# A bank for each transpose: q and k of the early chunks write to PSUM banks of their own

## The chip, the cores and the metric

The kernel runs on one core of a Trainium2 chip. The core has five engines with a queue of instructions each: TensorE (PE: matmuls and transposes, with its weight loads shown as PEld), VectorE (DVE), ScalarE (ACT), GpSimd (POOL) and SyncE (SP, which here only issues DMAs). Engines tell each other through semaphores. The metric is the device time of one execution in microseconds (us); less is better. PSUM, where TensorE writes, has eight banks in this kernel's book-keeping: five that the plan hands out one by one (bank 0 to bank 4), two for scores (the tile `sc`) and one for the state (the tile `st`).

## The reference

A gated linear attention feeds a two-layer block with a squared ReLU. Inputs are q, k, v and alpha of shape 4 x 8 x 768 x 48 (batch, heads, sequence, head dimension) and two weights, 384 x 2048 and 2048 x 384.

```python
for t in range(S):
    state = alpha[:, :, t, :, None] * state + np.einsum('bhd,bhe->bhde', k[:, :, t], v[:, :, t])
    y[:, :, t] = np.einsum('bhd,bhde->bhe', q[:, :, t], state)
x = y.transpose(0, 2, 1, 3).reshape(B * S, H * D)
h = x @ w_in
return (np.maximum(h, 0.0) ** 2) @ w_out
```

## The kernel before

**Tiles.** The 3072 tokens are cut into 24 chunks of 128 tokens, six to a batch element. The state is carried from one chunk to the next; within a chunk the recurrence is done with matmuls: cumulative sums of log alpha (`p0`), their exponentials `A` and `Ainv`, the products qA = q * A and kI = k * Ainv (L522, L528, L727), their transposes (`p1q` and `p1k`; in a double chunk `p1`), scores q k (`p2`) with a mask (`sm`), the state's update (`ps`, then `stm` and the copy `sb`), and the output (`p3a` from the old state, `p3b` from the scores), which is copied as `xn`, transposed once more (`p4`), and copied into `xT_big` as the input of the block. The block takes tokens in groups: the first of four chunks, two of one, then nine of two. `moe1` is x @ w_in with the ReLU on ACT (L915) and the square on DVE (L923); `moe2` is the product with w_out.

**Double chunks.** The first four chunks are done as two double chunks (`add_super`, L661): 256 tokens, in two halves of four heads each (v = 0 and 1). Each half has its own `p0`, products, transposes and copies. Chunks 4 to 23 are done one by one (`add_chunk`, L454). Chunks 4 and 5 (s below EARLY = 6) copy q and k out of PSUM with two instructions, either on ACT or on DVE; chunks 6 to 9 with one on DVE; from chunk 10 on the transposes are made by DMAs and take no PSUM.

**What sets the order.** Every step is an `Op` with an engine, a duration, the steps it depends on and a priority. `Plan.run` places them one at a time at the earliest time that its own durations give, and the instructions are then issued in the order of the planned starts. On the chip each engine goes through its queue in that order. An op may take a bank (`takes`) from a list of `Slots`; the bank comes free when the op in `gives` is done. The bank lists are `GLA_BANKS` (banks 0 and 1, for single chunks), `SUP_BANKS` (banks 0 to 3, for double chunks) and the last three for the block. Where the plan leaves TensorE idle before the first `moe2`, matmuls on a tile of zeros (`idle_mm`, tile `warm`) are put in.

**Around the change.** The four transposes of q and the four of k of one half (or of one chunk) each write 128 x 512 bf16 values, one kilobyte a partition, which is half of a bank; both go into one tile `pT` of 128 x 1024, a whole bank. q's are issued first, then k's. The copies (`cast`, L418, on ACT L420 and on DVE L422) bring each part to the tile `qkT`. The bank is given back by the copy of k. The semaphores are placed by the language's layer under the kernel: as built, the transposes of k wait for the copy of q where that copy was issued first, and the copy of q waits for the transposes of k where those were issued first.

Of the kernel before, what the change touches and what calls it, by code (L numbers as in the profile page):

```python
# [9 lines left out]
BF16 = mybir.dt.bfloat16  # L10
# [49 lines left out]
def after(op, x=0.0):  # L60
    return (op, x)
# [109 lines left out]
def kernel(  # L171
# [13 lines left out]
    P = 128  # L185
    DP = 64
    NP = H // 2
# [32 lines left out]
    HF = P // 2  # L220
# [46 lines left out]
    ident_bf = consts.tile([P, P], BF16)  # L267
# [6 lines left out]
    def pin(ins):  # L274
        tc.keep_in_program_order(ins)
# [4 lines left out]
    def tr(*a):  # L280
        pin(nc.tensor.transpose(*a))  # L281

    plan = Plan()
# [4 lines left out]
    GLA_BANKS = sl_bank[0:2]  # L288
    SUP_BANKS = sl_bank[0:4]
# [3 lines left out]
    def psum(op, shape, dt):  # L293
        i = op.slot.bank
        return banks[i].tile(shape, dt, name=f"bank{i}")
# [6 lines left out]
    def add(eng, dur, emit, *deps, **kw):  # L302
        return plan.add(Op(eng, dur, emit, deps, **kw))
# [69 lines left out]
    EARLY = 2 * 3  # L373
# [44 lines left out]
    def cast(op, out_t, in_t):  # L418
        if op.eng == "ACT":
            pin(nc.scalar.copy(out_t, in_t))  # L420
        elif op.eng == "DVE":
            pin(nc.vector.tensor_copy(out_t, in_t))  # L422
        else:
            pin(nc.gpsimd.tensor_copy(out_t, in_t))
# [29 lines left out]
    def add_chunk(s):  # L454
        d = C[s]
        b, c = divmod(s, NCH)
        i = s % NBUF
        L, qA, kI, ae = L_s[:, i], qA_s[:, i], kI_s[:, i], ae_s[:, i].rearrange("p j n -> p n j")
        was = C[s - NBUF]
        old = was["end"] if s < 2 * NS + NBUF else None  # L460
        g = dict(prio=-10.0 + s * 0.01)
# [68 lines left out]
        mk = d["use_kt"] = add("DVE", 0.47, e_kI, ai, d["ld_kt"], *([old] if old else [was["cps"][1], was.get("ps")]), **g)  # L530
# [4 lines left out]
                tr(d["pT"][:, p, :], qA[:, 2 * p:2 * p + 2, :], ident_bf)  # L535

        def e_p1k():
            for p in range(NP):
                tr(d["pT"][:, NP + p, :], kI[:, 2 * p:2 * p + 2, :], ident_bf)
        def e_turn():  # L540
            d["qkT"] = work.tile([P, 2 * NP, P], BF16, name="qkT")
            pin(nc.sync.dma_start_transpose(out=d["qkT"], in_=qk_s[:, i].rearrange("p x h d -> p (x h d)")))
        if s < XFROM:
            p1q = plan.add(Op("PE", 0.22, e_p1q, [mq], takes=GLA_BANKS, **g))
            p1k = plan.add(Op("PE", 0.22, e_p1k, [mk, after(p1q)], lat=0.15, **g))

        def e_cp(lo, hi):
            if lo == 0:
                d["qkT"] = work.tile([P, 2 * NP, P], BF16, name="qkT")
            cast(cpk if lo else cp, d["qkT"][:, lo:hi, :], d["pT"][:, lo:hi, :])  # L550
        if s < EARLY:
            cp = add({"ACT": 0.49, "DVE": 0.34}, 0, lambda: e_cp(0, NP), p1q, **g)
            cpk = add({"DVE": 0.34, "ACT": 0.49}, 0, lambda: e_cp(NP, 2 * NP), p1k, after(cp, -9.0), **g)
        elif s < XFROM:
            cp = cpk = add("DVE", 0.61, lambda: e_cp(0, 2 * NP), p1k, was["py_op"], **g)
        else:
            cp = cpk = add("XB", 0.0, e_turn, mq, mk, was["py_op"], lat=2.8)
            cp.turn = 1.2
        if s < XFROM:
            p1q.gives = cpk  # L560

        d.update(cps=[cp, cpk], mk=mk, vb_op=vb, ae1=ae1, kI=kI, ae=ae)
        if s < PAIRS:
# [97 lines left out]
    def add_super(u):  # L661

        d = SUP[u]
        i = 2 * u % NBUF
        pair = (C[2 * u], C[2 * u + 1])
        L, qA, kI, ae = L_s[:, i:i + 2], qA_s[:, i:i + 2], kI_s[:, i:i + 2], ae_s[:, i:i + 2].rearrange("p b j n -> p b n j")
        old = [C[2 * u - NBUF + ab].get("end") for ab in range(2)] if u >= 2 else []
        g = dict(prio=-10.0 + u * 0.02)
        any_ = (0, 1)
        sets = "p h s d -> p s h d"  # L670
        NH = NP // 2
# [54 lines left out]
        def e_mul(op, out, src, f):  # L726
            pin((nc.gpsimd if op.eng == "POOL" else nc.vector).tensor_mul(out, src, f))  # L727
        mq = [add("DVE", 0.47, lambda v=v: e_mul(mq[v], qA[:, :, hsl[v], 0:D], d["qt"][:, hsl[v]].rearrange(sets), d["A"][v]),
                  a_[v], d[f"ld_qt{v}"], *old, **g) for v in any_]
        mk = [add(KI_ON[u][v], 0, lambda v=v: e_mul(mk[v], kI[:, :, hsl[v], 0:D], d["kt"][:, hsl[v]].rearrange(sets), d["Ai"][v]),  # L730
                  ai[v], d[f"ld_kt{v}"], *old, **g) for v in any_]
        d["use_qt"], d["use_kt"] = mq[1], mk[1]

        d["pT"], d["qk"] = [None, None], [None, None]

        def e_p1(v, w, src):
            if w == 0:
                d["pT"][v] = psum(p1[v], [P, 2, NH, 2, 2, HF], BF16)
            for t in any_:
                for n in range(NH):  # L740
                    p = NH * v + n
                    tr(d["pT"][v][:, w, n, :, t, :], src[:, t, 2 * p:2 * p + 2, :], ident_bf)

        def e_cp(v, w):
            if w == 0:
                d["qk"][v] = work.tile([P, 2, NH, 2, 2, HF], BF16, name="qkT")
            cast((cpq, cp)[w][v], d["qk"][v][:, w], d["pT"][v][:, w])
        p1, cp, cpq = [None, None], [None, None], [None, None]
        for v in any_:
            p1[v] = plan.add(Op("PE", 0.225, lambda v=v: e_p1(v, 0, qA), [mq[v]], takes=SUP_BANKS, lat=0.15, **g))  # L750
            p1k = plan.add(Op("PE", 0.225, lambda v=v: e_p1(v, 1, kI), [mk[v], after(p1[v])], lat=0.15, **g))
            cpq[v] = add({"ACT": 0.49, "DVE": 0.34}, 0, lambda v=v: e_cp(v, 0), p1[v], **g)
            cp[v] = add({"DVE": 0.34, "ACT": 0.49}, 0, lambda v=v: e_cp(v, 1), p1k, cpq[v], **g)
            p1[v].gives = cp[v]
        cq = cp[1]

        def qT(p):
# [66 lines left out]
        for ab in any_:  # L824
            s = 2 * u + ab
# [40 lines left out]
            if s:  # L866
                p3a = c["p3a"] = plan.add(Op("PE", 0.2, e_p3a, [cq, before], takes=SUP_BANKS, **g))
            p3b = c["p3b"] = plan.add(Op("PE", 0.5, e_p3b, [*sm, *vb, after(p3a)], takes=None if s else SUP_BANKS,
                                         lat=0.15, **g))
# [140 lines left out]
    for x in DMA_ORDER + [s for s in range(2 * NS, NT) if s not in DMA_ORDER]:  # L1010
        if x in ("i", "o"):
            load_w(x)
        elif isinstance(x, str):
            for nm in x[1:].split():
                add_load2(int(x[0]), nm)
            if len(SUP[int(x[0])]) == 2 * len(srcs) - 1:
                add_super(int(x[0]))
        else:
            for nm, _ in srcs:
                add_load(x, nm)  # L1020
            add_chunk(x)
# [47 lines left out]
    for op in plan.order:  # L1069
        if op.eng == "PE":  # L1070
# [3 lines left out]
            if pe_end is not None and DUMMY:  # L1074
                cold = pe_end < COLD
                n = max(0, int((op.start - pe_end - (0.05 if cold else 0.2)) / (0.22 if cold else 0.11)))
# [32 lines left out]
```

## Time and profile before

| | |
|---|---|
| time, median of 3 runs | 178.14 us (178.06 to 179.42) |
| time of the profiled execution | 178.12 us |
| its span | 176.3 us |
| TensorE busy | 169.5 us, 96% of the span, 1854 matmuls |
| VectorE, ScalarE, GpSimd busy | 126.3, 123.1 and 53.4 us |
| granted TensorE clock | 0.999 |
| transposes of q and k on TensorE (L281) | 80, 219 ns each from start to result |
| copies of q or k, 128x512 | 10 on DVE, 422 ns each; 2 on ACT, 586 ns each |

The profile is one execution, read by the hardware profiler. Times of rows are counted from the start of the span. A row of the timeline has the start, the time from the first start to the last end of a run of equal instructions, the engine, the line, what is written and read, the number of instructions, and in brackets how long the engine was idle before and what ended that. A row of the waits has who waited, for whom, the total in us, how often, and the longest. The time of an execution is some 1.8 us more than its span.

### The profile page before, as it was taken

The page shows a single profiled execution, that of the slowest core. Times are in us where ns is not written, and L with a number is a line of the kernel's source. Part 1 is how long each engine was busy: PE and PEld are TensorE (multiplying, and loading weights), DVE is VectorE, ACT ScalarE, POOL GpSimd, SP SyncE. Part 2 cuts the span into 40 slices and gives each one's busy share as a digit, 9 for nine tenths or more (in the row PEclk, how much of TensorE's full clock was granted, in tenths as well). Part 3 has the DMA queues.
Part 4 walks back from the last instruction along what each step waited for, and adds up shares of the span by engine and source line. Part 5 has one row for each costly group of instructions (what it writes and reads, how often), then busy time and mean ns, then how long its engine had stood idle before and what let it go on. Part 6 is the DMA issues. An engine that isn't in the chain of part 4 may idle for free.

```text
span 176.3 us, 4803 instructions
## 1 busy us (share of the span) xinstructions
PE 169.5 (96%) x1854; PEld 125.0 (71%) x1854; DVE 126.3 (72%) x259; ACT 123.1 (70%) x266; POOL 53.4 (30%) x97
## 2 busy tenths in 40 slices
PE   7779999999999999999999999999999999999993
PEld 2457794566897788866786786785878866867863
DVE  6678889957799798869699777789486741820600
ACT  4569779446898679983899499695797833743821
POOL 6120779911121101032332213303328278200000
PEclk9999999999999999999999999999999999999999
DMA  5999999899989989999999996998989899822012
GB/s 132 274 283 301 382 387 369 175 224 204 223 176 179 212 163 179 179 179 214 199 168 214 178 199 135 142 226 152 192 157 196 215 199 325 306 45 93 0 45 89
DMA packets 117206, 34.86 MB, mean 198 GB/s; under 512 B 111952, under 2 KB 114640, under 8 KB 117184
## 3 DMA queue, kind: packets, MB, share of 16 engines
q1 hardware_dynamic: 115200, 31.21, 84.1%
q0 software_dynamic: 1984, 3.36, 6.2%
q8 instruction: 14, 0.23, 0.6%
q14 instruction: 8, 0.07, 0.1%
HBM read 25.17 MB, written 4.72 MB: 170 GB/s over the span
## 4 chain that ended last, share of the span: by engine, by line
PE 85%; DVE 6%; ACT 6%; issue 2%; DVEq 0%; ACTq 0%
PE bank L278 77%; PE bank L281 4%; PE sc L278 3%; PE st L278 2%; ACT r L915 2%; DVE sm L597 1%; DVE gT L923 1%; DVE qk_s L727 1%; ACT xn L420 1%; DVE qk_s L528 1%; ACT A L711 1%; DVE qkT L422 1%; ACT sb L847 1%; ACT Af L494 0%; ACT Ainv L711 0%
## 5 line engine op out<-in xcount | busy, mean ns | idle before, releaser
L278 PE MATMUL bank<-xT_big,w_in_b 128*128 128x256 bf16 (+2 forms) x606 | 72.2, 267 | 0.0
L278 PE MATMUL bank<-w_out_b,gT 128*128 128x384 bf16 (+2 forms) x400 | 68.8, 319 | 0.0
L915 ACT ACTIVATE r<-bank 128x512 bf16<-128x512 f32 (+1 forms) x97 | 56.5, 603 | 10.9 <-PE bank L278 8.6
L923 DVE TENSOR_TENSOR gT<-r 128x512 bf16<-128x512 bf16 (+1 forms) x97 | 47.2, 520 | 18.4 <-ACT r L915 17.9
L278 PEld LDWEIGHTS <-w_in_b 128*128 128x128 bf16 x606 | 53.3, 98 | 9.8
L278 PEld LDWEIGHTS <-gT 128*128 128x128 bf16 x400 | 37.4, 98 | 20.1
L470 POOL CAST vb<-vt 128x384 bf16<-128x384 f32 x20 | 10.6, 528 | 45.6 <-DMA vt<-in_v_dram 20.1
L991 ACT COPY held<-bank 128x384 f32<-128x384 f32 x21 | 10.1, 481 | 18.6 <-PE bank L278 17.3
L511 POOL DMA_DIRECT2D ae_s<-Af x24 | 12.1, 509 | 36.2 <-ACT Af L494 36.1
L597 DVE TENSOR_TENSOR sm<-sc,utri_b 128x512 bf16<-128x512 f32 x24 | 15.4, 683 | 2.8 <-PE sc L278 2.7
L525 DVE TENSOR_TENSOR qk_s<-qt,Af 128x384 bf16<-128x384 f32 x12 | 10.3, 856 | 6.4 <-ACT Af L494 6.3
L420 ACT CAST xn<-bank 128x384 bf16<-128x384 f32 x24 | 11.2, 484 | 4.7 <-PE bank L278 4.6
L278 PEld LDWEIGHTS <-qkT 64*128 64x128 bf16 (+2 forms) x304 | 10.6, 97 | 4.3 <-issue 1.9
L528 DVE TENSOR_TENSOR qk_s<-kt,Ainv 128x384 bf16<-128x384 f32 x20 | 11.7, 585 | 0.8 <-ACT Ainv L498 0.5
L465 ACT ACTIVATE L_s<-at 128x384 bf16<-128x384 f32 x20 | 10.7, 534 | 0.9 <-DMA at<-in_alpha_dram 0.9
L494 ACT ACTIVATE Af<-bank 128x384 f32<-128x384 f32 x12 | 10.6, 883 | 1.0 <-PE bank L278 0.5
L498 ACT ACTIVATE Ainv<-bank 128x384 bf16<-128x384 f32 x20 | 10.4, 519 | 0.0
L631 DVE TENSOR_TENSOR st<-st,ae_s 128x384 f32<-128x384 f32 x16 | 8.9, 558 | 1.9 <-ACT xn L420 1.1
L597 DVE TENSOR_TENSOR sm<-bank,utri_b 128x512 bf16<-128x512 f32 x16 | 10.2, 679 | 0.0
L281 PE MATMUL bank<-ident_bf,qk_s 128*128 128x128 bf16 x80 | 7.4, 219 | 2.5 <-DVE qkT L422 0.9
L422 DVE COPY qkT<-bank 128x512 bf16<-128x512 bf16 (+1 forms) x14 | 6.8, 497 | 4.2 <-PE bank L281 4.0
L636 ACT CAST sb<-st 128x384 bf16<-128x384 f32 x16 | 7.9, 497 | 2.5 <-DVE st L631 2.5
(74 smaller groups left out, 165.7 us busy)
## 6 DMA issues: line engine op xcount, KB each, us to landing
at<-in_alpha_dram SPq DMA_DIRECT2D x24, 192.0 KB, 3.9
qt<-in_q_dram SPq DMA_DIRECT2D x24, 192.0 KB, 3.8
kt<-in_k_dram SPq DMA_DIRECT2D x24, 192.0 KB, 3.9
vt<-in_v_dram SPq DMA_DIRECT2D x20, 192.0 KB, 3.8
wo<-in_moe_w_out_dram SPq DMA_DIRECT2D x4, 768.0 KB, 6.5
out_dram<-held POOLq DMA_DIRECT2D x13, 192.0 KB, 4.5
wi<-in_moe_w_in_dram SPq DMA_DIRECT2D x4, 384.0 KB, 6.5
wi<-in_moe_w_in_dram SPq DMA_DIRECT2D x2, 768.0 KB, 8.5
```

Source lines behind the costliest of these rows:

```text
L278: pin(nc.tensor.matmul(*a, **kw))
L281: pin(nc.tensor.transpose(*a))
L420: pin(nc.scalar.copy(out_t, in_t))
L465: pin(nc.scalar.activation(L[:, :, 0:D], d["at"], AF.Ln))
L470: pin(nc.gpsimd.tensor_copy(d["vb"], d["vt"]))
L494: pin(nc.scalar.activation(d["A"], split(d["pm"][:, 0:HD], s), AF.Exp))
L498: pin(nc.scalar.activation(d["Ai"], d["pm"][:, 0:HD].rearrange("p (h d) -> p h d", h=H), AF.Exp, scale=-1.0))
L511: pin(nc.gpsimd.dma_start(out=ae_s[HF * j:HF * j + D, i, j], in_=d["Af"][P - 1:P, j]))
L528: pin(nc.vector.tensor_mul(kI[:, :, 0:D], d["kt"], d["Ai"]))
L597: pin(nc.vector.tensor_mul(d["sm"][:, hh], d["sc"][hh], utri_b.to_broadcast([P, NP, P])))
L915: pin(nc.scalar.activation(box["r"][:, 0:w], box["ph"][:, 0:w], AF.Relu))
L923: pin(nc.vector.tensor_mul(gT[g][:, f0:f0 + per, lo * P:lo * P + n], r, r))
```

## The change

Transposes of q and transposes of k now take a bank each, in both double chunks and in chunks 4 and 5, and each bank is given back by its own copy. Chunks 6 to 9 keep one bank with one copy. The work, the engines' tiles and the number of matmuls are the same; the plan is run anew with the new banks.

```diff
@@ add_chunk: chunks 4 and 5 (s < EARLY)
         def e_p1k():
+            d["pTk"] = psum(p1k, [P, NP, P], BF16) if s < EARLY else d["pT"][:, NP:]
             for p in range(NP):
-                tr(d["pT"][:, NP + p, :], kI[:, 2 * p:2 * p + 2, :], ident_bf)
+                tr(d["pTk"][:, p, :], kI[:, 2 * p:2 * p + 2, :], ident_bf)
...
-            p1k = plan.add(Op("PE", 0.22, e_p1k, [mk, after(p1q)], lat=0.15, **g))
+            p1k = plan.add(Op("PE", 0.22, e_p1k, [mk, after(p1q)], takes=GLA_BANKS if s < EARLY else None, lat=0.15, **g))
...
-            cast(cpk if lo else cp, d["qkT"][:, lo:hi, :], d["pT"][:, lo:hi, :])
+            cast(cpk if lo else cp, d["qkT"][:, lo:hi, :], d["pTk"] if lo and s < EARLY else d["pT"][:, lo:hi, :])
...
         if s < XFROM:
-            p1q.gives = cpk
+            if s < EARLY:
+                p1q.gives, p1k.gives = cp, cpk
+            else:
+                p1q.gives = cpk
@@ add_super: the double chunks
-        d["pT"], d["qk"] = [None, None], [None, None]
+        d["pT"], d["qk"] = {}, [None, None]
 
         def e_p1(v, w, src):
-            if w == 0:
-                d["pT"][v] = psum(p1[v], [P, 2, NH, 2, 2, HF], BF16)
+            d["pT"][v, w] = psum((p1, p1k)[w][v], [P, NH, 2, 2, HF], BF16)
...
-                    tr(d["pT"][v][:, w, n, :, t, :], src[:, t, 2 * p:2 * p + 2, :], ident_bf)
+                    tr(d["pT"][v, w][:, n, :, t, :], src[:, t, 2 * p:2 * p + 2, :], ident_bf)
...
-            cast((cpq, cp)[w][v], d["qk"][v][:, w], d["pT"][v][:, w])
+            cast((cpq, cp)[w][v], d["qk"][v][:, w], d["pT"][v, w])
...
-            p1k = plan.add(Op("PE", 0.225, lambda v=v: e_p1(v, 1, kI), [mk[v], after(p1[v])], lat=0.15, **g))
+            p1k[v] = plan.add(Op("PE", 0.225, lambda v=v: e_p1(v, 1, kI), [mk[v], after(p1[v])], takes=SUP_BANKS, lat=0.15, **g))
...
-            p1[v].gives = cp[v]
+            p1[v].gives, p1k[v].gives = cpq[v], cp[v]
```

As built, TensorE's queue has the same instructions. Up to the output of the double chunks their order is the same. In chunk 5 the transposes of `xn` of chunk 4 come behind one quarter of `moe2` instead of ahead of it, a few matmuls of `moe1` move past transposes and outputs of chunks 5 and 6, and one copy of `xT_big` (chunk 4) goes to DVE instead of ACT. From about chunk 8 on all five queues have the order of before, with banks 0 and 1 exchanged. No DMA changes its place.

More of the change, by code (lines that the diff above doesn't have):

```diff
@@ L746, in e_cp @@
                 d["qk"][v] = work.tile([P, 2, NH, 2, 2, HF], BF16, name="qkT")
-            cast((cpq, cp)[w][v], d["qk"][v][:, w], d["pT"][v][:, w])
-        p1, cp, cpq = [None, None], [None, None], [None, None]
+            cast((cpq, cp)[w][v], d["qk"][v][:, w], d["pT"][v, w])
+        p1, p1k, cp, cpq = [None, None], [None, None], [None, None], [None, None]
         for v in any_:
             p1[v] = plan.add(Op("PE", 0.225, lambda v=v: e_p1(v, 0, qA), [mq[v]], takes=SUP_BANKS, lat=0.15, **g))
-            p1k = plan.add(Op("PE", 0.225, lambda v=v: e_p1(v, 1, kI), [mk[v], after(p1[v])], lat=0.15, **g))
+            p1k[v] = plan.add(Op("PE", 0.225, lambda v=v: e_p1(v, 1, kI), [mk[v], after(p1[v])], takes=SUP_BANKS, lat=0.15, **g))
             cpq[v] = add({"ACT": 0.49, "DVE": 0.34}, 0, lambda v=v: e_cp(v, 0), p1[v], **g)
-            cp[v] = add({"DVE": 0.34, "ACT": 0.49}, 0, lambda v=v: e_cp(v, 1), p1k, cpq[v], **g)
-            p1[v].gives = cp[v]
+            cp[v] = add({"DVE": 0.34, "ACT": 0.49}, 0, lambda v=v: e_cp(v, 1), p1k[v], cpq[v], **g)
+            p1[v].gives, p1k[v].gives = cpq[v], cp[v]
         cq = cp[1]
```

## The prediction, on record before the run

> **What bounds the kernel now.** I read the engines' shares first, then the waits of the first 22 us, then the timeline around each transpose of q and k. The page, shares by engine and the chain that ended last:
>
> ```profile
> PE 169.5 (96%) x1854; PEld 125.0 (71%) x1854; DVE 126.3 (72%) x259; ACT 123.1 (70%) x266; POOL 53.4 (30%) x97
> ...
> PE 85%; DVE 6%; ACT 6%; issue 2%; DVEq 0%; ACTq 0%
> ```
>
> TensorE is the bound. By stretches it is busy 7.51 of the first 10 us, 8.86 of the next 10, and from 20 to 170 us between 9.83 and 10 of every 10. So a microsecond saved ahead of 20 us moves the end only if TensorE reaches its dense part earlier; behind it, only true gaps of TensorE count. The waits, 0 to 22 us, name what the change touches:
>
> ```profile
> PE bank L281 <- DVE qkT L422: 0.9, 2, 0.5
> ...
> PE bank L281 <- ACT qkT L420: 0.7, 1, 0.7
> ```
>
> L281 are transposes, L422 and L420 the copies out of PSUM: three times in the double chunks the transposes of k stand behind the copy of q, 1.6 us in all. The timeline shows each, and what comes behind:
>
> ```profile
> 6.60 0.42 DVE L422 COPY qkT<-bank 128x512 bf16<-128x512 bf16 x1
> ...
> 7.07 0.38 PE L281 MATMUL bank<-ident_bf,qk_s 128*128 128x128 bf16 x4 [0.52 <-DVE qkT L422]
> ...
> 9.63 0.56 DVE L727 TENSOR_TENSOR qk_s<-kt,Ainv 128x384 bf16<-128x384 f32 x1
> ...
> 10.09 0.59 ACT L420 COPY qkT<-bank 128x512 bf16<-128x512 bf16 x1 [0.98 <-PE bank L281]
> ...
> 10.73 0.38 PE L281 MATMUL bank<-ident_bf,qk_s 128*128 128x128 bf16 x4 [0.67 <-ACT qkT L420]
> ...
> 17.05 0.38 PE L281 MATMUL bank<-ident_bf,qk_s 128*128 128x128 bf16 x4 [0.34 <-DVE qkT L422]
> ...
> 17.65 0.51 POOL L424 CAST vb<-vt 128x384 bf16<-128x384 f32 x1 [4.53 <-DMA vt<-in_v_dram]
> ...
> 18.35 0.51 PE L278 MATMUL st<-vb,qk_s 64*128 64x96 bf16 x8
> ```
>
> The reader is to see two kinds of edges: those between engines, which the change removes, and two that a DMA sets. The product kI of the second half starts at 9.63, and its load of k, issued at 4.66, took 4.9 us: it landed at 9.56. The load of v of the second double chunk, issued at 10.73, took 6.9 us; GpSimd had waited 4.53 us for it. In chunk 5 (timeline, 36 to 62 us) no transpose waits, but the copies do, and then TensorE:
>
> ```profile
> 44.13 0.75 DVE L422 COPY qkT<-bank 128x512 bf16<-128x512 bf16 x2 [0.91 <-PE bank L281]
> ...
> 45.00 0.10 PEld L278 LDWEIGHTS <-utri_b 128*128 128x128 bf16 x1 [0.48 <-PE bank L278]
> 45.03 0.32 PE L278 MATMUL bank<-L_s,utri_b 128*128 128x384 bf16 x1
> ```
>
> The row names TensorE's own matmul as releaser, which was long done. The bank that this p0 of chunk 6 takes is the one that the two copies empty at 44.88, so I take the copies.
>
> **The change part by part.**
>
> *First double chunk, first half.* kI is ready at 6.50 (row 5.95, 0.55), so the transposes of k start at some 6.60 instead of 7.07. Of these 0.47 us at most 0.07 outlive the load of k that lands at 9.56 and starts the second half's kI at 9.63. Worth nothing.
>
> *Second half.* kI ends at 10.19; k's transposes start at 10.26 instead of 10.73, their results are there at 10.65. The copy of k then waits for DVE, whose mask of 0.68 from 10.10 ends at 10.78: 10.78 instead of 11.22, **0.44 us** ahead. All that follows to 16.11 (state, sb, exponentials, products) hangs on this copy by the chain, and its loads land at 12.9 to 15.2, ahead of it.
>
> *Second double chunk.* In its second half the copy of q no longer stands ahead of k's transposes: kI ends at 16.66, TensorE is through with its matmuls at about the same time, so 16.75 instead of 17.05, **0.3 us** more. A wait is added: the transposes of xn of chunk 1 take the bank of the first half's q, whose copy ends at 16.19, against 16.04 before; behind them stand six moe1 matmuls of 0.055 us each and k's transposes. Its cost lies between 0 and 0.2 and is in the 16.75. So the scores come some 0.7 us earlier, and then v is missing: its cast ends at 17.65 + 0.51 = 18.16 whatever the transposes do. The state's matmuls start 0.05 behind such an end (sb ends at 20.17, its reader starts at 20.22), at 18.21 instead of 18.35. From 18.35 to 20.22 TensorE's queue is back to back (state, output, moe1, then the matmuls on zeros, which stay), so **0.14 us** is what TensorE takes along into its dense part; about 0.6 us turn into waiting for v.
>
> *Chunk 4.* Its eight transposes run back to back (38.55, 0.61) and TensorE has work ahead of the scores. Its k now takes the bank of its p0, last read at 37.89 (37.72 + 0.17). Nothing.
>
> *Chunk 5.* q's transposes start at 43.49, eight take 0.44 between starts; those of q alone give their last result at 43.49 + 3 x 0.055 + 0.219 = 43.88. The copy of q starts there + 0.03 = 43.91 instead of 44.13, both copies end 0.75 later at 44.66. Meanwhile TensorE does k, a quarter of moe2 (0.65, as from 42.84 to 43.49) and the moved transposes of xn: free at 44.75. p0 of chunk 6 follows the copies by 0.15 as before, at 44.81 instead of 45.03: **0.22 us**. Two waits are added. k's transposes wait for ACT's copy of xn (43.03 + 0.48 = 43.51), needed at 43.71: 0.2 us to spare. The copy of chunk 4's xT_big is now on DVE, behind both copies, and moe1 waits for it: xn's last result at 44.75 + 0.2, copy 0.35 (the mean of ten such), done at 45.33; moe1 is due at 44.81 + 0.34 + 0.33 = 45.48. Hidden with 0.15 to spare; uncovered, up to 0.35. Behind it on DVE are the masks, which start when the scores end, no sooner than 45.6.
>
> *Afterwards.* Orders are as before, no DMA moves. In the whole trace TensorE waits once for a load, 0.2 us, and loads from chunk 6 on land 0.1 to 10 us ahead of their readers, so I keep both gains to the end.
>
> Sum: 0.14 + 0.22 = 0.36. The profiled execution took 178.12 us (span 176.3), 0.02 under the median: **177.8 us**.
>
> A rule that speaks for more: the Trainium skill, page "Perfetto Trace Analysis", section "Optimizing Tensor Performance", says that independent groups of matmuls should go round different PSUM banks so that copying one out overlaps the next. Going by it alone, the 1.6 us of waits above and the gap in chunk 5 would go, some 1.9 us; the row of v's cast says why most of it can't.
>
> **The rivals.**
>
> *Nothing is left* (0.20): 178.1. The 0.14 disappears if v lands 0.1 us later, the 0.22 if p0 of chunk 6 has another reason, as its row's releaser allows. This is also what a change that doesn't unhook the transposes would give; as built, none of them waits for the other's copy.
>
> *More is left* (0.10): the 0.74 us are kept if v's cast isn't what holds the state, with the gap of 0.28 (TensorE free at 44.75, next start 45.03) gone whole: 1.0 us, **177.1**. Against it: GpSimd's wait ends on the DMA.
>
> *DVE gets too much* (0.16), slower: DVE is busy 5.00 of 5 us from 50 to 55, and 0.35 us of copy is moved to it from ACT. If it sets the pace there, its masks and squares come 0.35 later, less 0.14, and nothing of chunk 5's gain remains: +0.2, **178.3**; with xn's two new waits (0.2 each) up to 178.7. It decides once DVE has no idle time between the copy and 50 us. Against it: DVE stands idle 0.92 us ahead of the masks at 45.81, and the copy falls into that.
>
> *TensorE's clock falls* (0.02), slower: zeros at 1.06 run 7 in 3.17 us, 0.43 apart, three at 8.32 only 0.22 apart. A second slow stretch as long as the first (1.06 to 5.6) would cost half of 4.5 us: **180.4**. The page shows full clock in all slices, and the change takes gaps away. The Trainium skill, page "TensorE: Matmul & The Clock Gate", section "A second HAM failure mode: psum-queue depth-cycling", has a kernel that cycled through banks and fell back to the slow clock again and again; that speaks for this rival.
>
> **How the numbers follow.** Forecast 0.50 (177.5 to 178.0), nothing 0.20, more 0.10, DVE 0.16, clock 0.02, anything else 0.02. The range takes in all but clock and rest: 177.1 (all waits kept as gain) to 178.7 (new waits uncovered). One per cent is 1.8 us, about what a measurement of this kernel can tell from no change; no likely case reaches it. Faster by more: 0.03, for gains that add up behind 60 us; slower by more: 0.04, clock and rest.
>
> **What would show it.** Right: no wait of a transpose for a copy of q or k in the first 22 us; k's copy of the second half near 10.8; v's cast still at 17.65 with a longer wait ahead of the state's matmuls at 18.2; p0 of chunk 6 near 44.7 (45.03 less both gains); the end of TensorE 0.3 to 0.4 earlier. Wrong: the state's matmuls well ahead of 18.2, a gap at the moe1 behind p0 of chunk 6, DVE without idle time from 45 us on, or a slice of the clock under 9.

## The result, and the profile after

The changed kernel takes **177.94 us** (median of 19 runs), the kernel before, run in turn with it on the same chip, 178.5 us (median of 19). The ratio is 0.9955 with a 95% interval of 0.9937 to 0.9972: **0.8 us less, between 0.5 and 1.1**. That is 0.45%, well within one per cent. The ratio compares the means of the fast runs, 178.62 and 177.82 us, and leaves out one run of the changed kernel that took 180.86 us at a granted clock of 0.971; the medians differ by 0.56 us. The forecast was 0.36 us less and 177.8 us, from a profiled execution of 178.12 us; the kernel before turned out to take 178.5 as a rule, so the difference is what can be compared, not the time.

The profiled execution of the changed kernel took 178.0 us, span 176.2. The page, shares by engine and the chain that ended last:

```profile
PE 169.0 (96%) x1853; PEld 124.6 (71%) x1854; DVE 126.5 (72%) x260; ACT 122.4 (69%) x265; POOL 54.9 (31%) x97
...
PE 82%; DMA 6%; SPq 5%; ACT 3%; issue 1%; DVE 1%; ACTq 0%
```

TensorE bounds it as before. What is new is in the second line: the chain now leads through DMA (6%) and SyncE's queue of DMAs (5%), which had no share before. The waits of TensorE from 0 to 22 us (what waited, for what, us in total, times, longest):

```profile
PE bank L281 <- DVE qk_s L731: 1.4, 3, 0.6
...
PE st L278 <- ACT vb L420: 0.9, 1, 0.9
```

No transpose waits for a copy any more. They wait for their own product (qk_s, 0.9 us in the kernel before), and a new wait of 0.9 us stands in the list: the state's matmuls wait for the cast of v. That cast is done in two parts, on ScalarE and on GpSimd, which start within 0.1 us of each other; the rows below show GpSimd's. The timeline of the same stretch, with the rows that answer to those of before:

```profile
9.57 0.56 DVE L731 TENSOR_TENSOR qk_s<-kt,Ainv 128x384 bf16<-128x384 f32 x1 [0.19 <-DMA kt<-in_k_dram]
...
10.65 0.41 DVE L422 COPY qkT<-bank 128x512 bf16<-128x512 bf16 x1
...
16.11 0.39 PE L281 MATMUL bank<-ident_bf,qk_s 128*128 128x128 bf16 x4
...
17.82 0.51 POOL L424 CAST vb<-vt 128x384 bf16<-128x384 f32 x1 [4.77 <-DMA vt<-in_v_dram]
...
18.35 0.50 PE L278 MATMUL st<-vb,qk_s 64*128 64x96 bf16 x8 [0.86 <-ACT vb L420]
```

The first row is the product that waits for the load of k, which caps the gain of the first double chunk's first half (9.57; before 9.63). The copy of k comes at 10.65 instead of 11.22, the last transposes of k at 16.11 instead of 17.05: 0.94 us ahead. And then v is missing, as forecast: its cast starts at 17.82, and the state starts at 18.35, in this execution to the hundredth where it started before. Chunk 5:

```profile
43.90 0.76 DVE L422 COPY qkT<-bank 128x512 bf16<-128x512 bf16 x2 [0.68 <-PE bank L281]
...
44.71 0.10 PEld L278 LDWEIGHTS <-utri_b 128*128 128x128 bf16 x1
44.74 0.33 PE L278 MATMUL bank<-L_s,utri_b 128*128 128x384 bf16 x1
44.94 0.36 DVE L422 COPY xT_big<-bank 128x384 bf16<-128x384 bf16 x1 [0.28 <-PE bank L281]
...
45.51 1.29 DVE L601 TENSOR_TENSOR sm<-sc,utri_b 128x512 bf16<-128x512 f32 x2 [0.22 <-PE sc L278]
```

The copies of q and k start 0.23 earlier (44.13 before), the weights of p0 of chunk 6 are loaded without a wait (0.48 before), and p0 starts at 44.74 instead of 45.03. The copy that moved to VectorE stands at 44.94, with idle time before and behind it.

So at p0 of chunk 6 the one profile pair gives 0.29 us, and its two executions differ by 0.12 us in time (178.12 and 178.0); the runs give 0.8. The experiments look for the rest, and for what v does in other executions.

### The profile page after: what moved, and what is told of

The parts are those of the page before. It is cut to its first block, busy times and chain, and to the rows that moved or that the text cites. A ratio compares the mean times of both kernels' runs of the same rounds, so it can differ in the third digit from the quotient of the medians.

```text
span 176.2 us, 4802 instructions
## 1 busy us (share of the span) xinstructions
PE 169.0 (96%) x1853; PEld 124.6 (71%) x1854; DVE 126.5 (72%) x260; ACT 122.4 (69%) x265; POOL 54.9 (31%) x97
## 4 chain that ended last, share of the span: by engine, by line
PE 82%; DMA 6%; SPq 5%; ACT 3%; issue 1%; DVE 1%; ACTq 0%
PE bank L278 75%; SPq L415 5%; DMA vt<-in_v_dram 4%; PE bank L281 3%; PE st L278 2%; PE sc L278 2%; DMA at<-in_alpha_dram 2%; ACT r L918 2%; ACT xn L420 1%; SPq L338 1%; DVE qk_s L522 0%; ACT vb L420 0%; DVE qk_s L528 0%; DVE xT_big L422 0%; ACT L_s L465 0%
## 5 line engine op out<-in xcount | busy, mean ns | idle before, releaser
L470 POOL CAST vb<-vt 128x384 bf16<-128x384 f32 x20 | 12.0, 600 | 50.6 <-DMA vt<-in_v_dram 27.1
L498 ACT ACTIVATE Ainv<-bank 128x384 bf16<-128x384 f32 x20 | 10.4, 520 | 0.0
L354 POOL CAST w_in_b<-wi 128x768 bf16<-128x768 f32 x8 | 7.8, 998 | 5.2 <-DMA wi<-in_moe_w_in_dram 5.2
L278 PE MATMUL bank<-vb,sm 128*128 128x48 bf16 (+1 forms) x224 | 9.3, 182 | 0.0
```

Of the source, the lines that this page charges most:

```text
L278: pin(nc.tensor.matmul(*a, **kw))
L470: pin(nc.gpsimd.tensor_copy(d["vb"], d["vt"]))
L498: pin(nc.scalar.activation(d["Ai"], d["pm"][:, 0:HD].rearrange("p (h d) -> p h d", h=H), AF.Exp, scale=-1.0))
```

## The experiments

Every kernel is compared with the kernel before, run between the others on the same chip; ratios are to that.

### Each half of the change alone

The double chunks' half (in `add_super`), with chunks 4 and 5 as before:

```diff
-            if w == 0:
-                d["pT"][v] = psum(p1[v], [P, 2, NH, 2, 2, HF], BF16)
+            d["pT"][v, w] = psum((p1, p1k)[w][v], [P, NH, 2, 2, HF], BF16)
...
-            p1[v].gives = cp[v]
+            p1[v].gives, p1k[v].gives = cpq[v], cp[v]
```

> A bank for each transpose in the double chunks alone; chunks 4 and 5 as before. Theory (the load of v of the second double chunk holds the state's matmuls): the transposes come 0.5 to 0.9 us earlier up to 17 us, the state's matmuls at 18.35 stay, TensorE's dense part begins within 0.15 us of before, and p0 of chunk 6 has its gap of 0.28 us still; time 0 to 0.2 us under before. Rival (each removed wait is kept): 0.5 us or more under before.

Measured: 178.17 us, ratio 0.9975 (0.9955 to 0.9995), 0.45 us less (0.09 to 0.80). The expected 0 to 0.2 us and the rival's 0.5 both overlap that interval, so the time decides nothing; the rows say more. Its timeline:

```profile
16.99 0.51 POOL L424 CAST vb<-vt 128x384 bf16<-128x384 f32 x1 [3.96 <-DMA vt<-in_v_dram]
17.52 0.50 PE L278 MATMUL st<-vb,qk_s 64*128 64x96 bf16 x8
...
36.55 0.52 ACT L465 ACTIVATE L_s<-at 128x384 bf16<-128x384 f32 x1 [4.71 <-DMA at<-in_alpha_dram]
37.12 0.32 PE L278 MATMUL bank<-L_s,utri_b 128*128 128x384 bf16 x1 [1.36 <-ACT L_s L465]
...
45.79 0.10 PEld L278 LDWEIGHTS <-utri_b 128*128 128x128 bf16 x1 [0.48 <-PE bank L278]
```

In this execution v came 0.83 us earlier than in that of the changed kernel (16.99 against 17.82), and the state with it, at 17.52, 0.83 ahead of the kernel before. The same execution then lost all of it, and more: alpha of chunk 4 landed late, ScalarE's logarithm waited for it until 36.55, and TensorE for the logarithm, 1.36 us. In the last row, the weights of p0 of chunk 6 wait 0.48 us as in the kernel before: the gap of chunk 5 is untouched by this half.

The other half (in `add_chunk`), with the double chunks as before:

```diff
+            d["pTk"] = psum(p1k, [P, NP, P], BF16) if s < EARLY else d["pT"][:, NP:]
...
-            p1q.gives = cpk
+            if s < EARLY:
+                p1q.gives, p1k.gives = cp, cpk
```

> A bank for each transpose in chunks 4 and 5 alone; double chunks as before. Theory: all that the whole change brings comes from here, 0.3 us at p0 of chunk 6, and the rest of the 0.8 us measured from what it moves behind: time 0.3 to 0.8 us under before, the same as with the whole change within 0.2. Rival: the two parts bring half each, so 0.4 or less here and 0.4 in the double chunks alone.

Measured: 178.39 us, ratio 0.9988 (0.9971 to 1.0006), 0.2 us less. The expected 0.3 to 0.8 us, all that the whole change brings, was missed; the rival, some 0.4 us from each half, is nearer. Its timeline at chunk 5:

```profile
44.30 0.76 DVE L422 COPY qkT<-bank 128x512 bf16<-128x512 bf16 x2 [0.68 <-PE bank L281]
...
45.11 0.10 PEld L278 LDWEIGHTS <-utri_b 128*128 128x128 bf16 x1
45.14 0.33 PE L278 MATMUL bank<-L_s,utri_b 128*128 128x384 bf16 x1
```

With this half alone the wait of the weights is gone, though p0 itself comes no earlier than in the kernel before (45.14 against 45.03): this execution lost time further ahead, 0.26 us of it to a mask at 20.9 us. So the gap belongs to chunk 5's part of the change: it is there in the kernel before and with the other half alone, and away in both kernels that have this half. That part also changes TensorE's order, but not how much work stands between the transposes and p0; what it changes there is the start of the copies, 0.42 and 0.43 us behind q's first transpose with this half, 0.64 and 0.65 without. The two halves add up to 0.66 us, within the uncertainty of the 0.8 of the whole.

### v out of the way

If v holds the state of the second double chunk, more must be left of the change when v needn't be waited for. Both kernels, with the second double chunk using the first one's v:

```diff
+            if (u, nm) == (1, "vt"):
+                d[nm] = SUP[0][nm]
+                return
```

> Kernel before, but the second double chunk uses the v of the first one, which is there already; its load of v is left out, so its output is that of another v. This takes the wait for v away. Theory: without it the chain of waits through the transposes is what holds the state's matmuls, so they come only as early as the scores end, near 18.2 to 18.35; time within 0.3 us of before.

> Changed kernel, with the same load of v left out (the second double chunk uses the first one's v, so its output is that of another v). Theory: now the state's matmuls come 0.7 to 0.9 us earlier than in the kernel before with the same load left out, TensorE's dense part too, and the time is 1.0 to 1.6 us under that kernel's. Rival (something else, as the matmuls on zeros or the weights' casts, eats the double chunks' part): 0.3 to 0.8 us under it, as with the load.

Measured: 179.05 us for the kernel before so treated, ratio 1.0042 (1.0024 to 1.0059), and 177.93 us for the changed one, 0.9971 (0.9947 to 0.9995). Between the two the quotient is 0.9929, 1.3 us (give or take 0.5, from the two intervals). The state's matmuls of the former and then of the latter, from their timelines:

```profile
18.36 0.51 PE L278 MATMUL st<-vb,qk_s 64*128 64x96 bf16 x8
```

```profile
17.61 0.51 PE L278 MATMUL st<-vb,qk_s 64*128 64x96 bf16 x8
```

Without the load the kernel before starts its state at 18.36, against 18.35 with it: v was not what held it in that execution. The changed kernel starts 0.75 us ahead of it. That is what the transposes give once v has room, and it bears out the split of the forecast, some 0.7 us won of which v lets through a part. It is one execution of each. The times don't show what v is worth: the changed kernel is no faster without this load (0.9971) than with it (0.9955), and the 1.3 us come from the kernel before, which became slower by 0.7 us though it loads less. That is a miss; in its profile ScalarE's logarithms wait for late alphas, as in some below, but what made it slower was not settled.

### v later

The opposite: a load of 96 KB more in SyncE's queue ahead of this v, in both kernels, and the changed kernel itself on the same chip.

```diff
+            if (u, nm) == (1, "vt"):
+                extra = big.tile([P, 2, 2 * D], FP32, name="extra")
+                pin(nc.sync.dma_start(out=extra, in_=SRC2["kt"][0, u][:, 0:2]))
```

> The kernel before with one load more on SyncE's queue: 96 KB of k into a tile that nobody reads, issued right ahead of the second double chunk's load of v; nothing is left out. Theory (v, not the transposes, sets where the state of the second double chunk can start): v is issued some 0.7 to 1.3 us later and lands at 18.1 to 18.9 instead of 17.6, the state's matmuls start at 18.7 to 19.5 instead of 18.35, and the kernel takes 0.3 to 1.0 us more, 178.7 to 179.4. Rival (the transposes set it, v has room): state at 18.35, the time within 0.2 us of the kernel before.

> The changed kernel with the same extra load ahead of v. Theory: v lands at 18.1 to 19.0 as there, the state starts 0.05 us behind its cast in both kernels, so the double chunks' part of the gain is gone and only chunk 5's 0.2 to 0.3 us are left between the two: 178.4 to 179.1, 0.6 to 1.1 us over the changed kernel. Rival (the gain of the double chunks doesn't pass through v): the difference to the kernel before treated alike stays at 0.8 us or more.

> The changed kernel itself, as the reference for the other two on their chip. Both theories: 0.4 to 1.0 us under the kernel before there; v lands at 16.9 to 18.0 in its profile, as in the profiles seen so far, and the state's matmuls start within 0.7 us behind that.

Measured: 179.55 us, ratio 1.0026 (0.9997 to 1.0056), for the kernel before with the extra load; 178.42 us, 0.9983 (0.9953 to 1.0014), for the changed one; 177.71 us, 0.9955 (0.9922 to 0.9988), for the changed kernel as it is. The difference between the first two is 0.77 us and did not fall to the expected 0.2 to 0.3, though with an uncertainty of as much it can't be told from that. The timelines say why: the extra load did not do its work. The kernel before with the extra load:

```profile
17.99 0.51 POOL L427 CAST vb<-vt 128x384 bf16<-128x384 f32 x1 [4.95 <-DMA vt<-in_v_dram]
18.52 0.50 PE L278 MATMUL st<-vb,qk_s 64*128 64x96 bf16 x8 [0.25 <-ACT vb L423]
```

The changed kernel with the extra load, and then the changed kernel as it is, on the same chip:

```profile
17.73 0.51 POOL L427 CAST vb<-vt 128x384 bf16<-128x384 f32 x1 [4.54 <-DMA vt<-in_v_dram]
18.26 0.50 PE L278 MATMUL st<-vb,qk_s 64*128 64x96 bf16 x8
```

```profile
17.38 0.51 POOL L424 CAST vb<-vt 128x384 bf16<-128x384 f32 x1 [4.59 <-DMA vt<-in_v_dram]
17.91 0.50 PE L278 MATMUL st<-vb,qk_s 64*128 64x96 bf16 x8 [0.69 <-ACT vb L420]
```

v was issued at 12.0 and 12.1 us instead of 10.4 to 10.8, and yet its cast starts at 17.99 and 17.73, no later than in other executions. The time from issue to landing, 6.3 to 7.2 us in the executions that have this order of loads, shrank to 5.9 and 5.6. So this load's landing isn't set by when it is issued; that fits DMA engines that are behind with earlier loads (busy nine tenths or more in every slice of the changed kernel's page from 5 to 30 us), but how they share the work was not measured. The time comparison is therefore inconclusive on v. The rows are not: in the kernel before with v at 17.99, the state waits for v too (0.25 us), and starts 0.53 us behind the start of GpSimd's cast, as it does in the changed kernels. In the changed kernel with the extra load the row has no wait for v: there the last transposes of k started late, at 16.74, because a load of k was late, and TensorE was busy until 0.14 us ahead of the state.

### v earlier, in another order of loads

The changed kernel with the first load of w_in behind the loads of the second double chunk:

```diff
-    DMA_ORDER = ["0 at0 qt0 kt0 at1 vt qt1 kt1", "1 at0 at1", "i", "1 qt0 kt0 qt1 kt1 vt"] + ["i"] * 5 + ["o"] * 4
+    DMA_ORDER = ["0 at0 qt0 kt0 at1 vt qt1 kt1", "1 at0 at1", "1 qt0 kt0 qt1 kt1 vt"] + ["i"] * 6 + ["o"] * 4
```

> The changed kernel with the first load of w_in issued behind the loads of the second double chunk instead of ahead of them, so that this v is issued one place earlier. Theory (v's landing holds the state of the second double chunk, the transposes of it no longer do): v lands up to 0.8 us earlier, the state's matmuls start at 17.2 to 17.6 instead of 18.35, and the time is 0.3 to 0.8 us less than the changed kernel's 177.94, 177.2 to 177.6, if the w_in that is now behind is not missed. Rival (v's landing is chance, not its place in the queue, or w_in is then missing): 177.9 to 178.6.

Measured: 180.9 us, ratio 1.0137 (1.0102 to 1.0172): 2.4 us slower than the kernel before. Its timeline:

```profile
16.97 0.51 PE L278 MATMUL st<-vb,qk_s 64*128 64x96 bf16 x8
...
18.08 0.89 POOL L354 CAST w_in_b<-wi 128x768 bf16<-128x768 f32 x1 [1.97 <-DMA wi<-in_moe_w_in_dram]
...
152.63 0.60 PE L278 MATMUL bank<-xT_big,w_in_b 128*128 128x256 bf16 x4 [1.93 <-DMA xT_big<-xn]
```

v came early (its cast starts at 15.53) and the state at 16.97, earlier than in any other kernel. Then w_in was missing instead, and GpSimd waited 1.97 us for it. The planner also laid out the rest of the kernel anew, with a wait of 1.93 us for a transpose by DMA at 152 us that the others don't have. The run shows that the gain ahead of 17 us can be had and given back at the next load; it doesn't tell what the early v alone is worth.

### Late alphas

In the profile of the changed kernel, 0.45 us that it had won are lost at 116 us: p0 of chunk 19 is 0.73 us ahead of the kernel before (108.58 against 109.31), p0 of chunk 20 only 0.28 (116.94 against 117.22). Timeline:

```profile
116.00 0.52 ACT L465 ACTIVATE L_s<-at 128x384 bf16<-128x384 f32 x1 [0.35 <-DMA at<-in_alpha_dram]
116.43 0.46 ACT L420 CAST xn<-bank 128x384 bf16<-128x384 f32 x1
...
116.94 0.32 PE L278 MATMUL bank<-L_s,utri_b 128*128 128x384 bf16 x1 [0.29 <-ACT xn L420]
```

The logarithm waits 0.35 us for its alpha, the copy of xn stands behind it on ScalarE, and p0 of chunk 20 waits for the copy. Two experiments bear on it. First, both kernels with the loads of v of chunks 16 to 19 left out, so that there is less to bring ahead of these alphas:

```diff
+            if nm == "vt" and 16 <= s < 20:
+                d[nm] = C[14 + s % 2][nm]
+                return
```

> The kernel before, with the loads of v of chunks 16 to 19 left out (they use the v of chunks 14 and 15; the output is wrong in these four chunks), so that the DMA engines have 0.8 MB less to bring ahead of the alphas of chunks 20 to 23. Theory (what the change gains early is partly taken back where the alphas of chunks 20 to 23 land just when ScalarE wants them): the alphas land earlier, no wait of the logarithm for them at 115 to 130 us; the time is that of the kernel before or up to 0.3 us less, 178.1 to 178.5, for that kernel had 0.1 to 0.9 us of slack at these loads in its profile. Rival (the late alphas are chance and cost the kernel before as often as the changed one): 177.8 to 178.2, the same few tenths as in the changed kernel.

> The changed kernel with the same four loads of v left out. Theory: the 0.45 us that its profile lost between 113 and 117 us is kept, 177.3 to 177.6, and the difference to the kernel before treated alike grows from 0.8 to 0.9 to 1.2 us. Rival (the late alphas cost both kernels alike, so they have no part in the difference): the difference stays at 0.6 to 0.8 us. Second rival (nothing here hangs on these loads): 177.9, as the changed kernel itself.

Measured: 178.52 us, ratio 1.0007 (0.9981 to 1.0033), and 177.44 us, 0.9954 (0.9930 to 0.9978); the quotient is 0.9947, 0.95 us, give or take 0.6. In neither profile does a logarithm from 100 us on wait for an alpha, and the lead of 0.55 us at the output matmuls at 93 us (92.64 against 93.19) is still 0.54 at TensorE's end. The difference is what the theory gave (0.9 to 1.2) but can't be told from 0.8: the late alphas take a few tenths from single executions, of both kernels, and their part in the difference is too small for these runs.

Second, the changed kernel with the planner told that alphas from chunk 18 on take longer, so that the logarithms come later in ScalarE's order:

```diff
-        d["ld_" + nm] = add("DMA", LD if s < 12 else 0.95, ld, prev, lat=2.4)
+        d["ld_" + nm] = add("DMA", LD if s < 12 else 0.95, ld, prev, lat=3.4 if nm == "at" and s >= 18 else 2.4)
```

> The changed kernel in which the planner counts on 3.4 us instead of 2.4 us for the alpha loads of chunk 18 and later, so that their logarithms stand later in ScalarE's order and the copies of xn ahead of them. Theory (a logarithm that waits for a late alpha keeps the copy of xn behind it, and so the next p0, waiting): the 0.3 to 0.5 us lost at 116 us is kept, 177.4 to 177.7. Rival (the order then has its own gaps elsewhere, or the loss is in that one profile only): 177.8 to 178.2.

Measured: 177.54 us, ratio 0.9953 (0.9927 to 0.9978), against 0.9955 for the changed kernel. The 177.54 lies in the range that the theory gave only because the kernel before, too, is faster on this chip (178.27 us); as a ratio nothing is won, and the rival holds.

### One cast less

Between 45 and 93 us several profiles of the changed kernel win time where nothing was changed. VectorE and GpSimd there, in the kernel before, with the output matmuls that wait for the masks:

```profile
88.86 1.10 DVE L923 TENSOR_TENSOR gT<-r 128x512 bf16<-128x512 bf16 x1
89.15 0.52 POOL L470 CAST vb<-vt 128x384 bf16<-128x384 f32 x1
89.88 0.55 DVE L528 TENSOR_TENSOR qk_s<-kt,Ainv 128x384 bf16<-128x384 f32 x1
...
91.95 0.82 PE L278 MATMUL bank<-xT_big,w_in_b 128*128 128x256 bf16 x6
...
92.94 0.36 PE L278 MATMUL bank<-vb,sm 128*128 128x48 bf16 x8 [0.17 <-DVE sm L597]
```

The same in the changed kernel:

```profile
88.44 0.41 DVE L926 TENSOR_TENSOR gT<-r 128x512 bf16<-128x512 bf16 x1
88.75 0.52 POOL L470 CAST vb<-vt 128x384 bf16<-128x384 f32 x1
88.80 0.89 DVE L528 TENSOR_TENSOR qk_s<-kt,Ainv 128x384 bf16<-128x384 f32 x1
...
91.52 0.81 PE L278 MATMUL bank<-xT_big,w_in_b 128*128 128x256 bf16 x6
...
92.21 0.36 PE L278 MATMUL bank<-vb,sm 128*128 128x48 bf16 x8
```

The same two operations of VectorE take 1.10 and 0.55 us in the one, 0.41 and 0.89 in the other, by which of them the cast falls beside. The masks come late in the first, and TensorE waits: its output matmuls start 0.99 us behind the start of the six moe1 matmuls ahead of them, against 0.69 us in the second. That is a delay of 0.3 us. The row lists 0.17 of it as idle time; the rest is that the output matmuls of the second profile start 0.12 us before the last of the six ends (91.52 and 0.81). The test is the kernel before without this cast (chunk 15 then uses chunk 14's v):

```diff
+            if s == 15:
+                d["vb"] = C[14]["vb"]
+                return
```

> The kernel before without one instruction: GpSimd's cast of v of chunk 15, which stands at 89.15 us (chunk 15 uses the cast v of chunk 14, so its values are not those of the reference). In three profiles of the kernel before and its variants, TensorE then stands idle for 0.28 us ahead of the output matmuls at 92.9; in three of five profiles of the changed kernel it doesn't. Theory (the cast slows VectorE's operations that run beside it, so that the masks come late; which kernel escapes is a matter of which two overlap): the square at 88.9 takes 0.41 instead of 1.10 or 0.73 us, the product behind it 0.55, the gap at 92.9 is gone, and the time is 0.2 to 0.4 us less than that of the kernel before. Rival (the gap has another reason, or VectorE's times there don't depend on GpSimd): the gap of 0.28 stays and the time is within 0.1 us.

```profile
88.86 0.43 DVE L926 TENSOR_TENSOR gT<-r 128x512 bf16<-128x512 bf16 x1
89.23 0.56 DVE L531 TENSOR_TENSOR qk_s<-kt,Ainv 128x384 bf16<-128x384 f32 x1
...
92.62 0.36 PE L278 MATMUL bank<-vb,sm 128*128 128x48 bf16 x8
...
114.72 0.40 PE L278 MATMUL bank<-qkT 64*128 64x128 bf16 x8 [1.38 <-DMA qkT<-qk_s]
```

Without the cast the square takes 0.43 and the product 0.56, the output matmuls start 0.32 us earlier, and the wait is gone: the mechanism is shown in this profile. That it shortens the time is not: 180.11 us, ratio 1.0033 (0.9996 to 1.0070), with the kernel before at 179.52 on this chip, where 0.2 to 0.4 us less were expected. The profile loses 1.38 us again at 114 us, where a transpose by DMA is late.

## Why the prediction was right, and where it was short

The profiles put side by side tell more than the first pair. Starts in us of four steps that every kernel has, and the end of TensorE's last matmul. "v" is GpSimd's cast of v of the second double chunk, "state" the matmuls that need it, "p0" that of chunk 6, "output" the matmuls at 93 us. The variants are those of the experiments that have none of the change, or all of it, and that have the loads ahead of these steps in their old order and every cast; the two without v's load, the one with another order of loads and the one with one cast less are left out:

| kernel | v | state | p0 | output | end |
|---|---|---|---|---|---|
| before | 17.65 | 18.35 | 45.03 | 92.94 | 173.54 |
| before, four loads less | 17.76 | 18.52 | 45.20 | 93.19 | 173.78 |
| before, extra load | 17.99 | 18.52 | 45.19 | 93.12 | 174.53 |
| **mean** | 17.80 | 18.46 | 45.14 | 93.08 | 173.95 |
| changed | 17.82 | 18.35 | 44.74 | 92.21 | 173.45 |
| changed, again | 17.38 | 17.91 | 44.30 | 92.19 | 172.96 |
| changed, four loads less | 18.01 | 18.54 | 44.93 | 92.64 | 173.24 |
| changed, alphas planned later | 17.88 | 18.42 | 44.80 | 92.42 | 172.95 |
| changed, extra load | 17.73 | 18.26 | 44.65 | 92.25 | 173.50 |
| **mean** | 17.76 | 18.30 | 44.68 | 92.34 | 173.22 |

The means, unrounded, differ by 0.17 at the state, 0.46 at p0, 0.74 at the output matmuls, 0.73 at TensorE's end, and the means of the spans (176.97 and 176.12 us) by 0.85. So by these means the gain is made of about 0.17 in the double chunks, 0.29 in chunk 5 and 0.28 between 45 and 93 us, and nothing of it is lost behind that. These are eight executions; single ones scatter by several tenths, and only the 0.29 is the same in every one of them.

**The time: near, in part by luck.** The forecast was 177.8 and the median is 177.94. But the kernel before takes 0.36 us more than the execution that the forecast started from, and the change brings more than 0.36; the two misses partly cancel. What can be judged is the difference, and its terms.

**First double chunk, worth nothing ahead of 9.6, then 0.44: right, and a little short.** The load of k still starts kI of the second half (9.57), and the copy of k came 0.57 us earlier, at 10.65, where 10.78 was forecast: it did not wait for the end of VectorE's mask (10.05 and 0.68).

**Second double chunk, 0.7 us earlier of which 0.14 are kept: right in mechanism, near in size on the mean (0.17), wrong as a constant.** The transposes came 0.94 us earlier in the profiled execution. In all five profiles of the changed kernel and its variants, and in the one with the double chunks' half alone, the state starts 0.53 or 0.54 us behind the start of v's cast. In four of the six the state's row has a wait for v of 0.7 to 0.9 us: v holds it, as argued. In the other two (extra load, double chunks alone) no wait is listed, so v can cost little there. That the mean agrees with 0.14 is partly chance: the five starts of the state lie up to 0.63 us apart. But the step read v's arrival from one execution. The cast starts anywhere from 16.99 to 18.01, so what is kept runs from 0.83 (the double chunks alone) to nothing (the state at 18.54 in one of the profiles). With v out of the way, 0.75 us were kept at the state, in one pair. The rival "more is left" was this case taken to its end. The half alone measured 0.45 us (0.09 to 0.80), which takes in the 0.14.

**Chunk 4, nothing; chunk 5, 0.22: right in place, a little short.** The gap went whole, 0.29, as the rival "more is left" had it: from the state to p0 it is 26.67 or 26.68 us in the three profiles without the change and 26.38 or 26.39 in the five with it. The 0.15 us by which p0 was let follow the copies is what the forecast had too much: p0 now starts right behind TensorE's last transposes of xn, 0.08 us behind the copies' end (44.66). That the shared bank is behind the gap, and not the matmul that the row named, is shown by the two halves and by the start of the copies in them. The moved copy ended at 45.30 (44.94 and 0.36), forecast 45.33, and VectorE has 0.22 us idle between it and the masks: the rival in which VectorE gets too much falls.

**Afterwards, "I keep both gains to the end": the step that failed.** It was argued from slack that one execution showed (loads land 0.1 to 10 us ahead). In other executions the slack is used up: alpha of chunk 4 or of chunks 20 to 23, or a transpose by DMA, comes late and costs TensorE 0.3 to 1.4 us, with the change and without it. So the sign that was named, TensorE's end 0.3 to 0.4 us earlier, failed in the profile pair: it came 0.09 earlier, after a lead of 0.73 at 93 us. On the mean the late loads take as much from one group as from the other (from the output matmuls to the end it is 80.87 and 80.88 us), so they don't explain the difference. What the forecast lacked is the 0.28 us won behind chunk 5. What is won there comes mostly from the output matmuls at 93 us: from the start of the six moe1 matmuls ahead to theirs it is 0.93 to 0.99 us in all three profiles of the first group, 0.91 and 0.92 in two of the second and 0.66 to 0.69 in the other three, so the wait of about 0.3 is away in three of five. The experiment with one cast less shows what makes the wait. Why the changed kernel escapes it more often was not found: the two profiles of the second group that have it show the cast 0.31 and 0.32 us behind the start of VectorE's square, two that escape 0.29 and 0.31, and only in the third does the cast come clear of it (0.89). With five profiles it may be chance.

**The rivals.** "Nothing is left" is out: the interval ends at 0.5 us less. "TensorE's clock falls" is out as an effect of the change: the granted clock of the profiled execution is 1.000, and while one run with the change fell to 0.971 (180.86 us), so did one of the kernel before (181.19 us, in the runs beside the two halves). The Trainium skill's page "TensorE: Matmul & The Clock Gate", section "A second HAM failure mode: psum-queue depth-cycling", was cited for it; no profile here of a kernel with the change shows such a fall. The rule of the Trainium skill's page "Perfetto Trace Analysis", section "Optimizing Tensor Performance", to let independent groups go round the banks, gave 1.9 us by itself. The trace agrees in so far as the waits it names are all gone, and not in the amount: 0.46 us have arrived by chunk 6, since v's load stands behind the first of them.

## What to carry to other kernels

Undoing a wait is worth what the next one behind it leaves, and where that next one is a DMA, one profile gives only one draw of it: look at its landing in several executions before putting hundredths on it. Slack of a tenth at a load, read once, is no slack. A bank that is shared by two groups can cost even where no transpose waits, as in chunk 5: the copies start when the last group is done, and the next taker of the bank pays for it.

## What the runs showed of the hardware

**GpSimd beside VectorE.** A bf16 square of VectorE (128x512) takes 0.41 us alone and up to 1.10 beside GpSimd's cast of 0.52; an f32 product (128x384) takes 0.55 alone and 0.89 beside it. The Trainium skill's page "SBUF — State Buffer", section "SBUF: two separate sides", says that the two engines share a pair of ports, that a VectorE operation with two inputs in SBUF and a GpSimd operation that reads SBUF each hold it for a whole instruction while the other is blocked, and that it goes to the one that starts first. The trace agrees with the first part: in the kernel before, the square takes 0.69 us longer than alone, somewhat more than the whole cast, and ends at 89.96, 0.29 us behind the cast's end at 89.67. But by the rows the square had started first (88.86 against 89.15), so the order of starts that the profile shows doesn't agree with the last part. Nor is it always one that waits: in the kernel before with four loads less the square takes 0.74 and the cast 0.77 us, so both are stretched.

**A load's landing beside its issue.** Issuing v 1.3 to 1.7 us later, behind 96 KB more, left its cast within the range of the other executions.
